# The bias of a spectral layer, added by VectorE while it reads k from PSUM instead of by products on TensorE

## The chip, the cores and the metric

The kernel runs on one core of a Trainium2 chip. The metric is the device time of one execution in microseconds (us); lower is better. Before the change three runs took 1591.71, 1594.04 and 1594.58 us, median 1594.04.

## The reference

The kernel computes a spectral layer and a mixture of experts behind it. Of 8 batches with 2496 tokens of 256 channels, it takes the real Fourier transform along the tokens, multiplies the spectrum by a complex matrix, adds a complex bias, shrinks towards zero, transforms back, and sends each token through the one of 8 experts that its gate prefers. What matters here is the complex product with its bias:

```python
X = np.fft.rfft(x, axis=1)
Xr, Xi = (X.real.astype(np.float32), X.imag.astype(np.float32))
Yr = Xr @ w_r - Xi @ w_i + b_r
Yi = Xr @ w_i + Xi @ w_r + b_i
Yr = np.sign(Yr) * np.maximum(np.abs(Yr) - lam, 0.0)
Yi = np.sign(Yi) * np.maximum(np.abs(Yi) - lam, 0.0)
y = np.fft.irfft(Yr + 1j * Yi, n=x.shape[1], axis=1)
```

## The kernel before, in words

The Fourier transform of length 2496 is done in two steps of lengths 39 and 64 (`fwd_a`, `fwd_b`), with a turn through device memory between them (`spec_dram`), and the inverse likewise (`inv_b`, `inv_a`). Each batch's spectrum is cut into 10 pieces of 128 rows, so that the spectral stage has 80 iterations, one `mix` each (`spectral`, L399). The complex product is done with three real ones: k = (Xr + Xi) w_r, and two others with (w_i - w_r) and -(w_i + w_r), to which k is added. Each of them is made of six TensorE instructions of 256 columns in the type fp32r, because operands are split into a high and a low part (`sh`, `sl` from `halves`, L304; `wh`, `wl` from `split_constants`, L235).

In `mix` (L320), TensorE first makes the product pk in PSUM; ScalarE copies it to k in SBUF (L336); GpSimd copies one element of k to `mark` (L337), by which the scattering of finished rows to the experts is paced. Then TensorE makes the two others into one PSUM tile `pm`, each beginning with a bias product (L327): a 128x128 matrix of ones by a matrix whose row 0 holds the bias's high part and row 32 its low part, all else zero. VectorE adds `pm` and k (L343), with k repeated for the two parts. `shrink` (L346) makes the threshold out of the sum, u (the tile is called `v` in the trace).

pk lies in a ring of two PSUM buffers with the tag "yo" (`psi`), which it shares with `py`, the last product of the inverse transform (L394), and with small products of the routing (`pr`, `pn`, `pq`). `pm` and `pb`, the product of `fwd_b`, have one PSUM buffer each; k has one buffer in SBUF.

The order on TensorE, on SP's queue and, within the spectral loop, on ScalarE and VectorE is the order in which the program is written. In one iteration (L441 to L492) that is: `fwd_b` and the first part of `halves` for the piece behind, the first part of `shrink` for the piece before, the second part of `halves`, routing work (`tick`), the first part of `mix` (pk and k), `fwd_a` of the next batch, `shrink`'s second and third part with routing work between them, and the second part of `mix` (`pm` and u). In four of ten iterations (`turning`, the third to the sixth of a batch) the inverse's last step `inv_a` runs in three places of the iteration, and k comes behind `fwd_a`:

```python
            if turning:
                next(mix)
            next(small, None)
            self.tick(2 + spare)
            inverse()
```

`tick` takes up the next steps of `route` (L546), some 30 small VectorE operations per half batch, and of `table` (L626). In the last batch `spare` is 1, and more of them are taken in each iteration.

Of the kernel before, what the change touches and what calls it, by code (L numbers as in the profile page):

```python
# [10 lines left out]
F32 = mybir.dt.float32  # L11
F32R = mybir.dt.float32r
# [12 lines left out]
D = 256  # L25
# [73 lines left out]
class Kernel:  # L99
# [80 lines left out]
    def open_forward(self, st):  # L180
        tc, nc, nb = self.tc, self.nc, self.nb
        f = self.f = self.pool(st, "f", 1, side="right")
        self.xp = self.pool(st, "xp", 5, side="right")
        self.tp = self.pool(st, "tp", 6, side="right")
        self.w = self.pool(st, "w", 2, side="right")
        self.psf = self.pool(st, "psf", 1, side="right", space=PSUM)

        self.far = far = f.tile([117, 120], F32, name="far")
        self.fer = f.tile([78, 120], F32, name="fer")
        nc.sync.dma_start(far, self.c_fa)  # L190
        nc.sync.dma_start(self.fer, self.c_fe)
        self.bm = f.tile([128, K1, 128], F32, name="bm")
        self.bi = f.tile([128, K1, 128], F32, name="bi")
        self.bias = f.tile([128, 2, D], F32R, name="bias")
        self.ones = f.tile([128, 128], F32R, name="ones")
        self.xg = {}
        for q in range(6):
            self.load_x(0, q)
        nc.sync.dma_start(self.bm[:, 0:4, :], self.c_bm[:, 0:4, :])
        raw = {}  # L200
        for nm, src in (("r", self.w_r), ("i", self.w_i)):
            raw[nm] = self.w.tile([128, 2, D], F32, tag="v", name="wraw")
            nc.sync.dma_start(raw[nm], src.rearrange("(c p) n -> p c n", p=128))
        self.wh, self.wl = {}, {}
        self.raw = raw
        self.braw = self.w.tile([33, 2, D], F32, tag="y", name="braw", bufs=6)
        for h, b in ((0, self.b_r), (1, self.b_i)):
            for q in (0, 32):
                nc.gpsimd.dma_start(self.braw[q:q + 1, h, :], b.rearrange("(o n) -> o n", o=1))
        self.nlam = f.tile([128, 1], F32, name="nlam")  # L210
        nc.vector.memset(self.nlam, -LAM)

        nc.gpsimd.dma_start(self.gar, self.c_ga)
        for c in range(2):
            nc.gpsimd.dma_start(self.iw[:, c, c * 128:c * 128 + 8], self.w_gate[c * 128:(c + 1) * 128, :])
        nc.gpsimd.dma_start(self.ids, self.c_ids)
        nc.gpsimd.dma_start(self.score, self.c_score)
        nc.gpsimd.dma_start(self.base, self.c_base)
        nc.gpsimd.dma_start(self.ltri_f, self.c_ltri)
        nc.gpsimd.dma_start(self.tcol, self.c_tcol)  # L220
        nc.gpsimd.memset(self.z[:, :, 64:66, :], 0.0)
# [13 lines left out]
    def split_constants(self):  # L235
        nc, f, raw = self.nc, self.f, self.raw
        ws = self.w.tile([128, 2, D], F32, tag="r", name="wsum")
        wd = self.w.tile([128, 2, D], F32, tag="r", name="wdif")
        nc.vector.tensor_sub(wd, raw["i"], raw["r"])
        nc.vector.scalar_tensor_tensor(out=ws, in0=raw["i"], scalar=-1.0, in1=raw["r"], op0=ALU.mult, op1=ALU.subtract)  # L240
        raw = {"r": raw["r"], "d": wd, "s": ws}
        zero = self.w.tile([128, 2, D], F32, tag="y", name="zero", bufs=6)
        nc.vector.memset(zero, 0.0)
        nc.vector.tensor_copy(self.bias, zero)
        nc.vector.tensor_scalar_add(self.ones, zero[:, 0, 0:128], 1.0)
        bh = self.w.tile([33, 2, D], F32R, tag="y", name="bh", bufs=6)
        nc.scalar.copy(self.bias[0:1], self.braw[0:1])
        nc.scalar.copy(bh[32:33], self.braw[32:33])
        nc.vector.tensor_sub(self.bias[32:33], self.braw[32:33], bh[32:33])
        for nm in ("s", "d", "r"):  # L250
            self.wh[nm] = f.tile([128, 2, D], F32R, name="wh" + nm)
            self.wl[nm] = f.tile([128, 2, D], F32R, name="wl" + nm)
            nc.scalar.copy(self.wh[nm], raw[nm])
            nc.vector.tensor_sub(self.wl[nm], raw[nm], self.wh[nm])
        nc.scalar.copy(self.gh, self.gar)
        nc.vector.tensor_sub(self.gl, self.gar, self.gh)
        for c in range(2):
            nc.vector.tensor_copy(self.iw[:, c, 8 - 8 * c:136 - 8 * c], self.ident)
        nc.vector.tensor_copy(self.ltri, self.ltri_f)
# [60 lines left out]
    def mix(self, b, s):  # L320
        nc = self.nc
        sh, sl = self.ss.pop((b, s))

        def product(nm, slot, to):
            i = 0 if nm == "r" else 1
            if i:
                nc.tensor.matmul(to, self.ones, self.bias[:, 1 if nm == "d" else 0, :], start=True, stop=False)  # L327
            for c in range(2):
                for a, ww in ((sh, self.wh), (sh, self.wl), (sl, self.wh)):
                    nc.tensor.matmul(to, a[:, c, slot, :], ww[nm][:, c, :], start=i == 0, stop=i == (5 if nm == "r" else 6))  # L330
                    i += 1

        pk = self.psi.tile([128, 512], F32, tag="yo", name="pk")
        product("r", 2, pk[:, :D])
        k = self.w.tile([128, D], F32, tag="k", name="k", bufs=1)
        nc.scalar.copy(k, pk[:, :D])  # L336
        self.paced = nc.gpsimd.tensor_copy(self.mark, k[0:1, 0:1])  # L337
        yield
        p = self.psf.tile([128, 2, D], F32, tag="m", name="pm", bufs=1)
        product("d", 0, p[:, 1, :])  # L340
        product("s", 1, p[:, 0, :])
        u = self.w.tile([128, 2, D], F32, tag="v", name="v")
        nc.vector.tensor_add(u, p, k.unsqueeze(1).broadcast_to((128, 2, D)))  # L343
        self.us[b, s] = u

    def shrink(self, b, s):  # L346
# [52 lines left out]
    def spectral(self, fwd):  # L399
# [41 lines left out]
        for it in range(n):  # L441
# [28 lines left out]
            if not turning:  # L470
                next(mix)
            for a in first[it]:
                self.fwd_a(*a)
            if turning:
                next(mix)
# [3 lines left out]
            next(small, None)  # L479
            self.tick(1 + spare)  # L480
            next(mix, None)
            inverse()
            self.tick(1 + spare)
# [474 lines left out]
```

## Time and profile before

| | |
|---|---|
| median of three runs | 1594.04 us (1591.71 to 1594.58) |
| profiled execution | 1596.27 us, span 1594.4 us |
| granted TensorE clock, mean | 0.987 of 2.4 GHz |
| TensorE, recorded as busy | 1531.1 us |
| VectorE | 1245.3 us |
| ScalarE | 1077.7 us |
| GpSimd | 529.1 us |

Busy time is a union of the recorded intervals; matmuls are pipelined and overlap, so TensorE's share says little of how near it is to its own rate, and the distance of starts has to be read. PE is TensorE's matmul, PEld its weight load, DVE is VectorE, ACT ScalarE, POOL GpSimd. In a row of the timeline, what stands in brackets is the idle time of the engine before that instruction, and what ended it.

### The profile page before, as it was taken

The page shows a single profiled execution, that of the slowest core. Times are in us where ns is not written, and L with a number is a line of the kernel's source. Part 1 is how long each engine was busy: PE and PEld are TensorE (multiplying, and loading weights), DVE is VectorE, ACT ScalarE, POOL GpSimd, SP SyncE. Part 2 cuts the span into 40 slices and gives each one's busy share as a digit, 9 for nine tenths or more (in the row PEclk, how much of TensorE's full clock was granted, in tenths as well). Part 3 has the DMA queues.
Part 4 walks back from the last instruction along what each step waited for, and adds up shares of the span by engine and source line. Part 5 has one row for each costly group of instructions (what it writes and reads, how often), then busy time and mean ns, then how long its engine had stood idle before and what let it go on. Part 6 is the DMA issues. An engine that isn't in the chain of part 4 may idle for free.

```text
span 1594.4 us, 35844 instructions
## 1 busy us (share of the span) xinstructions
PE 1531.1 (96%) x10963; PEld 1409.5 (88%) x10963; DVE 1245.3 (78%) x2680; ACT 1077.7 (68%) x2257; POOL 529.1 (33%) x462
## 2 busy tenths in 40 slices
PE   5999999999989798899999999999999999999997
PEld 2899898999979787789999999999999999999996
DVE  2577687777757786878888888888888888888886
ACT  2677777777756566566767676767676767676765
POOL 3002432415141433713232323333333332333332
PEclk8999999999999999999999999999999999999999
DMA  8843554636352314243213123213123213223110
GB/s 266 231 139 114 170 150 130 181 110 202 109 158 86 94 35 123 74 111 98 49 48 101 45 48 97 49 48 97 48 48 96 48 49 96 50 55 88 45 48 20
DMA packets 182962, 153.55 MB, mean 96 GB/s; under 512 B 120474, under 2 KB 154176, under 8 KB 182509
## 3 DMA queue, kind: packets, MB, share of 16 engines
q1 hardware_dynamic: 162829, 107.17, 25.9%
q0 software_dynamic: 19936, 44.04, 8.4%
q8 instruction: 89, 1.46, 0.4%
q14 instruction: 108, 0.88, 0.2%
HBM read 243.07 MB, written 66.37 MB: 194 GB/s over the span
## 4 chain that ended last, share of the span: by engine, by line
issue 41%; PE 32%; POOL 18%; DVE 4%; ACT 2%; DMA 2%; POOLq 0%; SPq 0%; another core or an unknown queue 0%; DVEq 0%; ACTq 0%
POOL out L881 17%; PE pm L330 7%; PE pz L380 5%; PE pb L300 4%; PE pv L369 4%; PE py L394 4%; PE pa L276 4%; PE pk L330 3%; PE pm L327 1%; DMA wraw<-w_r 1%; POOL xs_dram L612 1%; DVE y L356 0%; DMA x<-x 0%; POOLq L881 0%; ACT yb L395 0%
## 5 line engine op out<-in xcount | busy, mean ns | idle before, releaser
L881 POOL DMA_INDIRECT out<-o,row x154 | 299.0, 1942 | 577.3 <-DVE o L879 537.4
L871 PE MATMUL po<-h,hh 128*128 128x512 f32 x1312 | 462.4, 396 | 0.1
L833 PE MATMUL ph<-xh,h 128*128 128x256 f32 x1312 | 373.3, 285 | 6.0 <-issue 2.5
L833 PE MATMUL ph<-xh,l 128*128 128x256 f32 x1312 | 372.8, 284 | 1.0 <-DVE l L774 0.7
L833 PE MATMUL ph<-xl,h 128*128 128x256 f32 x1312 | 372.3, 284 | 0.0
L838 ACT ACTIVATE hh<-ph 128x512 fp32r<-128x512 f32 x328 | 195.9, 598 | 240.7 <-PE ph L833 230.2
L839 DVE SCALAR_TENSOR_TENSOR hl<-ph,hh 128x512 fp32r<-128x512 f32 x328 | 226.7, 691 | 139.8 <-ACT hh L838 126.9
L868 PE MATMUL po<-h,hl 128*128 128x256 f32 x1148 | 322.2, 281 | 0.2 <-DVE hl L839 0.2
L871 PEld LDWEIGHTS po<-h,hh 128*128 128x128 f32 x1312 | 241.6, 188 | 44.7 <-ACT hh L838 0.4
L833 PEld LDWEIGHTS ph<-xh,h 128*128 128x128 f32 x1312 | 252.1, 192 | 7.5 <-issue 3.2
L833 PEld LDWEIGHTS ph<-xh,l 128*128 128x128 f32 x1312 | 252.4, 192 | 5.3 <-DVE l L774 1.1
L833 PEld LDWEIGHTS ph<-xl,h 128*128 128x128 f32 x1312 | 252.3, 192 | 0.0
L868 PEld LDWEIGHTS po<-h,hl 128*128 128x128 f32 x1148 | 217.4, 189 | 4.3 <-DVE hl L839 0.5
L774 DVE TENSOR_TENSOR l<-r,h 128x512 fp32r<-128x512 f32 x332 | 206.9, 684 | 4.0 <-DMA xr<-xs_dram 1.7
L789 DVE TENSOR_TENSOR h<-r,h 128x512 fp32r<-128x512 f32 x332 | 207.1, 684 | 1.1 <-ACT h L788 0.9
L612 POOL DMA_INDIRECT xs_dram<-yb,pos x176 | 179.9, 1022 | 82.5 <-issue 59.3
L773 ACT CAST h<-r 128x512 fp32r<-128x512 f32 x332 | 180.8, 618 | 2.8 <-DMA r<-moe_w 2.8
L788 ACT CAST h<-r 128x512 fp32r<-128x512 f32 x332 | 180.5, 618 | 0.6 <-DMA r<-moe_w 0.6
L337 POOL COPY mark<-k 1x1 f32<-1x1 f32 x80 | 24.4, 305 | 356.1 <-ACT k L336 352.5
L356 DVE SCALAR_TENSOR_TENSOR y<-v,r 64x256 f32<-64x256 f32 x320 | 133.7, 418 | 6.1 <-ACT r L350 1.6
L313 DVE TENSOR_TENSOR su<-re,pb 128x256 f32<-128x256 f32 x80 | 33.7, 421 | 93.5 <-ACT sh L312 49.4
L380 PE MATMUL pz<-iw,z 128*120 128x136 f32 x704 | 97.1, 281 | 4.5 <-DVE zl L386 3.7
(180 smaller groups left out, 2861.1 us busy)
## 6 DMA issues: line engine op xcount, KB each, us to landing
r<-moe_w SPq DMA_DIRECT2D x178, 512.0 KB
r<-moe_w SPq DMA_DIRECT2D x632, 128.0 KB
spec_dram<-ae SPq DMA_DIRECT2D x88, 240.0 KB
t<-spec_dram SPq DMA_DIRECT2D x160, 128.0 KB
xq<-xs_dram SPq DMA_DIRECT2D x312, 64.0 KB
x<-x SPq DMA_DIRECT2D x40, 384.0 KB
x<-x SPq DMA_DIRECT2D x40, 84.0 KB
xs_dram<-yb,pos POOLq DMA_INDIRECT x176
```

Source lines behind the costliest of these rows:

```text
L380: nc.tensor.matmul(p[:120, c * 136:(c + 1) * 136], self.z[:, c, 3 * g:3 * g + 3, :].rearrange("p j a -> p (j a)"), self.iw[:, c, :], start ...
L612: i = nc.gpsimd.indirect_dma_start(out=self.xs[:, :], out_offset=bass.IndirectOffsetOnAxis(ap=pos[:n, g:g + 1], axis=0), in_=y[:n, g, 0:XW ...
L773: nc.scalar.copy(hi[:, c, s], v)
L774: nc.vector.tensor_sub(lo[:, c, s], v, hi[:, c, s])
L788: nc.scalar.copy(hi[:, s, :], v)
L789: nc.vector.tensor_sub(lo[:, s, :], v, hi[:, s, :])
L833: nc.tensor.matmul(p[:, i, :], a[:, c, f * 128:(f + 1) * 128], v[:, c, :], start=m == 0, stop=m == 5)
L838: nc.scalar.activation(hh[:, s, :], p, AF.Relu)
L839: nc.vector.scalar_tensor_tensor(out=hl[:, s, :], in0=p, scalar=0.0, in1=hh[:, s, :], op0=ALU.max, op1=ALU.subtract)
L868: nc.tensor.matmul(p[:, :D], hl[:, f - 1, hs], w2[:, f - 1, 0, :], start=False, stop=False)
L871: nc.tensor.matmul(p, hh[:, f, hs], w2[:, f].rearrange("p a d -> p (a d)"), start=f == 0, stop=f == 7)
L881: i = nc.gpsimd.indirect_dma_start(out=self.out[:, :], out_offset=bass.IndirectOffsetOnAxis(ap=at[h], axis=0), in_=o[:, h, :], in_offset=N ...
```

## The change

The bias is laid out over all 128 partitions as a 128 x 2 x 256 tile by two DMAs that repeat a row. The bias products and the matrix of ones are gone, with what prepared them. VectorE reads pk from PSUM, repeated for the two parts, adds the bias tile, and writes a k of two parts; ScalarE's copy is gone. The later addition of `pm` and k reads the two-part k.

```diff
-        self.bias = f.tile([128, 2, D], F32R, name="bias")
-        self.ones = f.tile([128, 128], F32R, name="ones")
+        self.bias = f.tile([128, 2, D], F32, name="bias")
...
-        self.braw = self.w.tile([33, 2, D], F32, tag="y", name="braw", bufs=6)
         for h, b in ((0, self.b_r), (1, self.b_i)):
-            for q in (0, 32):
-                nc.gpsimd.dma_start(self.braw[q:q + 1, h, :], b.rearrange("(o n) -> o n", o=1))
+            nc.gpsimd.dma_start(self.bias[:, h, :], b.rearrange("(o n) -> o n", o=1).broadcast_to((128, D)))
...
-        zero = self.w.tile([128, 2, D], F32, tag="y", name="zero", bufs=6)
-        nc.vector.memset(zero, 0.0)
-        nc.vector.tensor_copy(self.bias, zero)
-        nc.vector.tensor_scalar_add(self.ones, zero[:, 0, 0:128], 1.0)
-        bh = self.w.tile([33, 2, D], F32R, tag="y", name="bh", bufs=6)
-        nc.scalar.copy(self.bias[0:1], self.braw[0:1])
-        nc.scalar.copy(bh[32:33], self.braw[32:33])
-        nc.vector.tensor_sub(self.bias[32:33], self.braw[32:33], bh[32:33])
...
         def product(nm, slot, to):
-            i = 0 if nm == "r" else 1
-            if i:
-                nc.tensor.matmul(to, self.ones, self.bias[:, 1 if nm == "d" else 0, :], start=True, stop=False)
+            i = 0
             for c in range(2):
                 for a, ww in ((sh, self.wh), (sh, self.wl), (sl, self.wh)):
-                    nc.tensor.matmul(to, a[:, c, slot, :], ww[nm][:, c, :], start=i == 0, stop=i == (5 if nm == "r" else 6))
+                    nc.tensor.matmul(to, a[:, c, slot, :], ww[nm][:, c, :], start=i == 0, stop=i == 5)
                     i += 1
...
-        k = self.w.tile([128, D], F32, tag="k", name="k", bufs=1)
-        nc.scalar.copy(k, pk[:, :D])
-        self.paced = nc.gpsimd.tensor_copy(self.mark, k[0:1, 0:1])
+        k = self.w.tile([128, 2, D], F32, tag="k", name="k", bufs=1)
+        nc.vector.tensor_add(k, pk[:, :D].unsqueeze(1).broadcast_to((128, 2, D)), self.bias)
+        self.paced = nc.gpsimd.tensor_copy(self.mark, k[0:1, 0, 0:1])
...
-        nc.vector.tensor_add(u, p, k.unsqueeze(1).broadcast_to((128, 2, D)))
+        nc.vector.tensor_add(u, p, k)
```

On VectorE, in the fourth iteration with `inv_a` of the third batch, where the routing's running sums (`scan`, `sb`) stand; before:

```order
L317 TENSOR_TENSOR sl<-su,sh 128x2x128
L582 TENSOR_TENSOR scan_101<-scan_100 117x88
L582 TENSOR_TENSOR scan_102<-scan_101 117x88
L582 TENSOR_TENSOR scan_101<-scan_102 117x88
L582 TENSOR_TENSOR scan_102<-scan_101 117x88
L588 CAST sb<-scan_102 117x8
L356 SCALAR_TENSOR_TENSOR y<-v,r 64x256 x2
L386 TENSOR_TENSOR zl<-pz,zh 120x272 x2
```

and in the changed kernel (its line numbers are lower by up to 13):

```order
L306 TENSOR_TENSOR sl<-su,sh 128x2x128
L569 TENSOR_TENSOR scan_101<-scan_100 117x88
L569 TENSOR_TENSOR scan_102<-scan_101 117x88
L569 TENSOR_TENSOR scan_101<-scan_102 117x88
L569 TENSOR_TENSOR scan_102<-scan_101 117x88
L575 CAST sb<-scan_102 117x8
L323 TENSOR_TENSOR k<-pk,bias 128x512
L343 SCALAR_TENSOR_TENSOR y<-v,r 64x256 x2
L373 TENSOR_TENSOR zl<-pz,zh 120x272 x2
```

The addition that makes k stands behind the routing's five operations and ahead of `y`.

On ScalarE, the same place before, where the copy stood behind `ae`, the copy of `fwd_a`'s product:

```order
L350 ACTIVATE r<-v,nlam 128x512
L316 CAST sh<-su 128x2x128
L284 COPY ae<-pa 120x512
L336 COPY k<-pk 128x256
L385 CAST zh<-pz 120x272 x2
```

In the changed kernel the row of k is missing there, and the others stand as they did.

On VectorE in the last batch, second iteration, the changed kernel's k stands behind the sums of the tile table (the last of them is shown):

```order
L648 TENSOR_TENSOR te<-tcol,pfb 128x8
L651 TENSOR_REDUCE fin<-te 128x1
L323 TENSOR_TENSOR k<-pk,bias 128x512
L343 SCALAR_TENSOR_TENSOR y<-v,r 64x256 x2
L653 TENSOR_SCALAR fin<-fin 128x2
```

Before, `y` followed `fin` there, and k was made on ScalarE.

## Rows read from the trace of the kernel before

**Rows 1.** The page, share of busy time and number of instructions of each engine over the whole span.

```profile
PE 1531.1 (96%) x10963; PEld 1409.5 (88%) x10963; DVE 1245.3 (78%) x2680; ACT 1077.7 (68%) x2257; POOL 529.1 (33%) x462
```

**Rows 2.** Busy time by stretch of the span: the stretch in us, its length, busy us of PE, PEld, DVE, ACT and POOL (with the number of instructions), then granted TensorE clock, the DMA engines' share and GB/s. The beginning, the third batch, and the last.

```profile
0.00:40.00 40.00, 23.45 (x69) 10.46 (x70) 11.24 (x30) 9.21 (x16) 12.37 (x29) 0.84 0.83 267
...
170.00:241.00 71.00, 70.13 (x541) 64.31 (x540) 53.46 (x148) 51.47 (x127) 24.86 (x33) 1.00 0.50 149
...
529.00:605.00 76.00, 64.70 (x507) 61.07 (x508) 58.29 (x183) 45.41 (x112) 29.00 (x37) 0.98 0.18 55
```

**Rows 3.** Timeline of TensorE in the fourth iteration with `inv_a` of the third batch: start in us, length in us, instruction. First the end of pk, then the second `py`, then the first and the last of fourteen `pm` products in a row.

```profile
207.31 0.29 PE L330 MATMUL pk<-whr,sl 128*128 128x256 f32 x1
...
208.74 0.29 PE L394 MATMUL py<-zh,gh 120*117 120x272 f32 x1
...
209.11 0.29 PE L327 MATMUL pm<-bias,ones 128*128 128x256 f32 x1
...
210.66 0.28 PE L330 MATMUL pm<-whs,sl 128*128 128x256 f32 x1
```

**Rows 4.** Timeline of VectorE in a plain iteration, the second one of the third batch.

```profile
170.46 0.69 DVE L343 TENSOR_TENSOR v<-pm,k 128x512 f32<-128x512 f32 x1 [1.00 <-PE pm L330]
172.23 0.42 DVE L313 TENSOR_TENSOR su<-re,pb 128x256 f32<-128x256 f32 x1 [1.08 <-ACT sh L312]
...
175.47 0.69 DVE L343 TENSOR_TENSOR v<-pm,k 128x512 f32<-128x512 f32 x1 [0.26 <-issue]
177.24 0.42 DVE L313 TENSOR_TENSOR su<-re,pb 128x256 f32<-128x256 f32 x1 [1.08 <-issue]
```

**Rows 5.** Timelines of TensorE and VectorE in the last batch: the places where TensorE begins after an idle time, and what stands on VectorE there.

```profile
546.45 0.58 PE L394 MATMUL py<-zh,gh 120*117 120x272 f32 x1 [5.37 <-ACT k L336]
...
547.40 0.84 DVE L356 SCALAR_TENSOR_TENSOR y<-v,r 64x256 f32<-64x256 f32 x2
...
568.07 0.38 PE L394 MATMUL py<-zh,gh 120*117 120x272 f32 x1 [0.72 <-ACT k L336]
...
577.73 0.39 PE L394 MATMUL py<-zh,gh 120*117 120x272 f32 x1 [0.18 <-DVE rb L598]
...
588.15 0.17 PE L592 MATMUL pr<-sb,ltri 117*117 117x8 bf16 x1 [1.43 <-DVE sb L588]
...
589.01 0.69 DVE L343 TENSOR_TENSOR v<-pm,k 128x512 f32<-128x512 f32 x1
589.62 0.41 DVE L313 TENSOR_TENSOR su<-re,pb 128x256 f32<-128x256 f32 x1
```

**Rows 6.** Groups of instructions of VectorE and ScalarE from 45 to 605 us: line, engine, operation, tiles, shapes, number, then busy us and mean ns of one, then idle us of the engine before them and what ended it.

```profile
L343 DVE TENSOR_TENSOR v<-pm,k 128x512 f32<-128x512 f32 x80 | 55.1, 689 | 37.9 <-PE pm L330 18.8 <-issue 4.6 <-PE pz L380 4.5
...
L313 DVE TENSOR_TENSOR su<-re,pb 128x256 f32<-128x256 f32 x78 | 32.8, 421 | 80.8 <-ACT sh L312 36.7 <-PE pz L380 26.5 <-ACT re L311 8.0
...
L336 ACT COPY k<-pk 128x256 f32<-128x256 f32 x79 | 33.6, 426 | 3.6 <-remote 2.0 <-PE pk L330 1.0 <-PE pz L380 0.4
```

**Rows 7.** Timeline of ScalarE around k, in the third and then in the fourth iteration with `inv_a` of the third batch.

```profile
198.41 0.28 ACT L562 ACTIVATE ex<-lg 117x88 f32<-117x88 f32 x1 [1.22 <-DVE lg L560]
198.59 0.57 ACT L284 COPY ae<-pa 120x512 f32<-120x512 f32 x1
199.06 0.38 ACT L336 COPY k<-pk 128x256 f32<-128x256 f32 x1
...
207.74 0.38 ACT L336 COPY k<-pk 128x256 f32<-128x256 f32 x1
```

**Rows 8.** Timeline of VectorE in the fourth iteration with `inv_a` of the third batch.

```profile
207.74 1.10 DVE L582 TENSOR_TENSOR scan<-scan 117x88 f32<-117x88 f32 x4
208.87 0.17 DVE L588 CAST sb<-scan 117x8 bf16<-117x8 f32 x1
208.95 0.84 DVE L356 SCALAR_TENSOR_TENSOR y<-v,r 64x256 f32<-64x256 f32 x2
```

**Rows 9.** Timelines in the third iteration with `inv_a` of the third batch: VectorE's last `lg`, and the second `py` on TensorE.

```profile
198.13 0.25 DVE L560 TENSOR_TENSOR lg<-lg,mx 117x88 f32<-117x88 f32 x1
...
199.49 0.38 PE L394 MATMUL py<-zh,gh 120*117 120x272 f32 x1 [0.76 <-ACT k L336]
```

**Rows 10.** Timelines of VectorE and TensorE in the eighth and ninth iteration of the third batch. Between the first and the last of its rows VectorE has no row with an idle time in brackets.

```profile
220.43 0.42 DVE L313 TENSOR_TENSOR su<-re,pb 128x256 f32<-128x256 f32 x1 [1.09 <-PE pk L330]
...
225.50 0.68 DVE L343 TENSOR_TENSOR v<-pm,k 128x512 f32<-128x512 f32 x1
...
226.66 0.17 DVE L588 CAST sb<-scan 117x8 bf16<-117x8 f32 x1
...
231.66 0.42 DVE L313 TENSOR_TENSOR su<-re,pb 128x256 f32<-128x256 f32 x1 [0.92 <-ACT re L311]
...
227.80 0.17 PE L592 MATMUL pr<-sb,ltri 117*117 117x8 bf16 x1
...
227.88 0.37 PE L327 MATMUL pm<-bias,ones 128*128 128x256 f32 x1
```

**Rows 11.** Timeline of GpSimd at the beginning, and the summary of ScalarE's k over the whole span (length of one in ns, least, median and greatest; first and last start).

```profile
1.36 0.71 POOL L209 DMA_DIRECT2D braw<-b_r  x1 [0.40 <-issue]
...
2.99 0.97 POOL L209 DMA_DIRECT2D braw<-b_i  x2
...
L336 ACT COPY k<-pk x80: 353/446/474, 42.9 to 604.4; 128x256 f32<-128x256 f32 x80
```

## The prediction

> **What bounds the kernel now.** I read the page's shares of busy time first [rows 1], then the same by stretch [rows 2], then TensorE's and VectorE's instructions in order of time, last the waits. The change touches the spectral stage alone, about 45 to 605 us of the span of 1594.4: `mix` runs there, 80 times. In an undisturbed batch (170 to 241 us) TensorE's records cover 70.13 of 71 us, VectorE's 53.46, ScalarE's 51.47 [rows 2]. Busy shares of overlapping matmuls prove little, so I looked at starts: in the run of `pm` products the first starts at 209.11 and the fourteenth at 210.66, thirteen steps of 0.119 us without a hole, although each is recorded as 0.28 us [rows 3]. TensorE works through its queue at its own rate; VectorE and ScalarE catch up in gaps, as the 1.0 us and 1.1 us before `v` and `su` [rows 4]. So in most of the stage time is TensorE's. The exception is the last batch, 529 to 605 us: TensorE covers only 64.70 of 76 us while VectorE has 58.29 [rows 2], and TensorE is seen waiting for it [rows 5].
>
> **The change, part by part.**
>
> *Removed from TensorE:* 160 bias products, two in each `mix`. They are worth their spacing, not their recorded length: 160 x 0.119 = **19.0 us** gained, 0.238 in each iteration [rows 3]. The granted clock is 1.00 in that stretch, the 2.4 GHz level [rows 2]. The Trainium skill (TensorE: Matmul & The Clock Gate, "Wait — 56ns, not 53.3ns?") gives the columns over 2.4 GHz plus 2.5 ns, which for 256 columns I estimate as 109 ns: 17.5 us in place of 19.0, and 1.5 us less gain in the sum; the row shows 0.119, so it decides.
>
> *Moved from ScalarE to VectorE:* k. ScalarE loses 80 copies of 0.43 us; VectorE gains 80 additions. No row has this very operation. The nearest is `v<-pm,k`, the same 128x512 with one operand in PSUM and one repeated: 689 ns [rows 6], and I take that, since the output count and the two operands agree. The lower end is 421 ns, `su`, also an addition from PSUM but over 256 (if the repeated reading cost nothing); the upper end is two such, 842 ns. What the next VectorE instruction sees is less than the recorded length: `v` starts at 589.01 and the next at 589.62, so 0.61 us of the engine [rows 5]. 80 x 0.61 = 49 us more for VectorE. Where does that lie? In a plain iteration VectorE idles 0.26 + 1.08 us between 172.23 and 177.24 [rows 4], a period of 5.01 us that the removed products shorten by 0.24; 0.61 + 0.24 fits under 1.34. There I cost it at nothing; its cover is this idle time, and if that were gone each iteration would cost up to 0.61.
>
> *Who waits for k.* k reads pk out of a ring of two PSUM buffers ("yo") that `py` also uses. In the four iterations of a batch in which `inv_a` runs, pk takes one, the first `py` behind it the other, and the second `py` waits until k has read pk. That is the place where the position in a queue decides:
> - Fourth of those iterations: ScalarE made k at 207.74 to 208.12 [rows 7] and the second `py` at 208.74 needed no wait [rows 3]. VectorE now has k behind four `scan` additions and the cast `sb`, so it can begin at 208.95, where `y` began [rows 8], and ends at 208.95 + 0.69 = 209.64; `py` starts about 0.05 later (as after ScalarE's k, which ended at 199.44, for 199.49 [rows 7, 9]), 209.69 in place of 208.74: 0.95 us lost, in six batches **5.7 us**. With the ends above, 4.1 to 6.6.
> - Third: ScalarE's k was held by `ex` and `ae` until 199.06, and `py` waited 0.76 us for it [rows 7, 9]. VectorE's k follows `lg` and ends at 198.38 + 0.69 = 199.07, not 199.44: 0.37 us gained, six times, **2.2 us**.
> - First and second: k's end moves by under 0.2 us; nothing.
>
> *The busiest plain iterations* (seventh to ninth of a batch, with the routing work): VectorE has no gap from 220.43 to 231.66 but the 0.92 us at the end [rows 10]. Two ks add 1.22 us there, and TensorE moves up 0.24 to 0.48. `sb` would end at 226.83 + 0.61 = 227.44, and TensorE wants it at 227.80 - 0.24 = 227.56 [rows 10]: just in time. Cost 0, bound 0.6 per batch. This is the thinnest margin of the forecast.
>
> *Last batch:* two routing jobs and the tile table share it, with more of them in each iteration, and TensorE already waits. k now follows the table's sums and ends at 547.40 + 0.69 = 548.09, where `py` got it at 546.45: 1.7 us. In the next three marked places it ends or pushes what TensorE waits for (k itself, `rb`, `sb`) by about 0.6 each [rows 5]. Together **3.5 us** lost; ends 0 (these waits are absorbed) and 7 (VectorE's ten ks at 0.61 plus part of the first again).
>
> *Beginning:* four DMAs of 1 KB into two rows become two that repeat 256 numbers over 128 partitions, 256 KB; four small VectorE operations, two ScalarE copies go. The bias is needed first at about 42.9 us, its DMAs are issued at 1.36 to 3.96 [rows 11]. Cost 0; the upper bound is the 256 KB at the rate of that stretch, 267 GB/s [rows 2], 1.0 us. One fewer row on GpSimd is nothing; its `mark` now reads VectorE's k, which only shifts when three rows may be scattered, and the scatters have room.
>
> *ScalarE* is relieved of 34 us [rows 6]; no wait of TensorE ends on it there but the k above, so I add nothing.
>
> **Sum:** -19.0 + 5.7 - 2.2 + 3.5 = -12.0 us. The profiled execution took 1596.27 us, so 1584.3; the median of the runs shown is 1594.04, 2.2 lower, so I say **1582.0 us**. The expert stage behind is not touched and moves up as a block.
>
> **Rivals.**
> A. *No new waits.* VectorE always arrives in time: -19.0 - 2.2 = -21.2, 1572.8 us. For it: the gaps of the plain iterations [rows 4]. Against: the order on VectorE in the fourth iteration leaves no way around `scan`.
> B. *VectorE's queue becomes the pace* where routing work is queued: seventh to ninth iteration of six batches and the ten of the last, 28 iterations, each paying 0.61 instead of gaining 0.24. 28 x 0.61 = +17.1, the other 52 gain 12.4, the two `py` terms are +5.7 - 2.2: +8.2, **1602.2 us**, slower. It decides if VectorE's 0.92 us of idle time [rows 10] is used up and the delay reaches the single PSUM buffer of `pm`, which `v` must have read before the next `pm`. For it: 1.22 us do not fit in 0.92. Against: the iterations behind have gaps of over 1 us, and `pm` begins more than 1 us after the `v` before it. The Trainium skill (Perfetto Trace Analysis, "Optimizing Scalar/DVE Operations") advises moving work from VectorE to ScalarE when VectorE is saturated, and this change does the opposite; by that rule B is the outcome, while the trace agrees only in 529 to 605 us.
> C. *No gain.* What TensorE saves it waits again at the next hand-over, as at the end of a `pm` whose `v` comes later: about 1594. Against it are the hole-free starts [rows 3].
>
> One thing hangs over all: TensorE stood still 5.37 us at 546.45 for no reason of the program's order [rows 5]. Such a pause may come or go, so I widen by about one on either side.
>
> **How the numbers follow.** Forecast 0.58, A 0.13, B 0.20, C 0.09. About 0.2% (3.2 us) is what a measurement of this kernel can tell from no change. Faster by over that: forecast nearly whole, and A: 0.70. Within: C and the edges of the forecast: 0.13. Slower: B less its better edge: 0.17. The forecast's own range is 1575 to 1590 (the ends of its terms); with A below and most of B above, 1573 to 1600.
>
> **What would show it.** Right: no `bias` product, `pm` groups of 12; the k addition near 0.69 us; in 170 to 241 us the period shorter by about 1.8 us; a TensorE wait of about 1 us for k at the fourth `inv_a` iteration, none of 0.76 at the third; the last batch no shorter. Wrong: TensorE waits for `v` or `sl` in plain iterations (B), the batch shortened by the full 2.4 (A), or not at all (C).

## The result, and the profile of the changed kernel

The changed kernel took 1602.27 us (median of 7 runs, 1596.88 to 1607.15), the kernel before 1592.27 us beside it (7 runs): a ratio of 1.0063, 95% interval 1.0041 to 1.0085, **slower by 10 us**. I had said 1582.0 and 0.70 for faster. The profiled execution took 1605.27 us, with a span of 1603.4.

The edit took the bias products out and moved k. On the page (columns as in [rows 1]) TensorE has 160 products fewer:

```profile
PE 1519.4 (95%) x10803; PEld 1390.0 (87%) x10803; DVE 1288.3 (80%) x2756; ACT 1057.0 (66%) x2175; POOL 536.8 (33%) x460
```

In the groups from 45 to 605 us (columns as in [rows 6]) k takes 685 ns, near the 0.69 us that I had taken:

```profile
L323 DVE TENSOR_TENSOR k<-pk,bias 128x512 f32<-128x512 f32 x80 | 54.8, 685 | 3.6 <-PE pm L317 2.3 <-PE pa L265 0.7 <-PE pk L317 0.4
```

The timelines of TensorE and VectorE in the third and fourth iterations with `inv_a` of the third batch answer to [rows 3, 7 to 9]. The wait of 0.76 us at the third is down to 0.31; I had said 0.37 less, it is 0.45 less. At the fourth there is a new one, but for `yb`, ScalarE's copy, and not for k:

```profile
198.14 0.68 DVE L323 TENSOR_TENSOR k<-pk,bias 128x512 f32<-128x512 f32 x1
198.88 0.39 PE L381 MATMUL py<-zh,gh 120*117 120x272 f32 x1 [0.31 <-DVE k L323]
208.10 0.69 DVE L323 TENSOR_TENSOR k<-pk,bias 128x512 f32<-128x512 f32 x1
208.52 0.39 PE L381 MATMUL py<-zh,gh 120*117 120x272 f32 x1 [0.47 <-ACT yb L382]
```

What I had not foreseen stands in the stretches (columns as in [rows 2]). In 168 to 173 us VectorE works 0.98 and ScalarE 0.61 of 5 us; in 598 to 617 us, at the end of the loop, TensorE only 9.07 of 19:

```profile
168.00:173.00 5.00, 5.00 (x40) 4.51 (x38) 0.98 (x2) 0.61 (x2) 2.71 (x3) 1.00 0.85 247
598.00:617.00 19.00, 9.07 (x62) 7.14 (x62) 7.91 (x18) 7.30 (x14) 12.57 (x14) 0.87 0.26 80
```

VectorE's and TensorE's timelines there show the largest hole: the last product of `pm` starts at 603.36, `v` waits until 614.11, and `pv` behind it starts after 7.65 us of TensorE's idle time; the `pv` before it had waited 2.13.

```profile
603.36 0.28 PE L317 MATMUL pm<-whs,sl 128*128 128x256 f32 x1
...
604.17 0.69 DVE L323 TENSOR_TENSOR k<-pk,bias 128x512 f32<-128x512 f32 x1 [2.27 <-PE pm L317]
604.78 1.73 DVE L343 SCALAR_TENSOR_TENSOR y<-v,r 64x256 f32<-64x256 f32 x4
614.11 0.69 DVE L330 TENSOR_TENSOR v<-pm,k 128x512 f32<-128x512 f32 x1 [7.61 <-remote]
...
616.65 2.05 PE L356 MATMUL pv<-bi,y 128*128 128x128 f32 x8 [7.65 <-DVE y L343]
```

The kernel before has such holes too, elsewhere. I compared the start of each iteration's first pk product in both traces: after 15 iterations the changed kernel is 2.5 us ahead, after 60 it is 5.1 behind, after 65, where two holes of before have passed, 3.0 ahead, after 79 1.5 behind, and at the first expert product 10.1 behind.

Three theories follow. **Theory 1**: VectorE's order makes TensorE wait in the loop, more than forecast. **Theory 2**: these pauses decide, in which VectorE and ScalarE stand though TensorE goes on; in the profiles they lie where GpSimd scatters rows one behind the other, 0.3 us apart, and the change may move those runs together, since `mark` now follows VectorE's k. **Theory 3**: VectorE's k is held because its single buffer must first be read by `mark`, behind those rows.

### The profile page after: what moved, and what is told of

It is laid out like the page before. It is cut to its first block, busy times and chain, and to the rows that moved or that the text cites. A ratio compares the mean times of both kernels' runs of the same rounds, so it can differ in the third digit from the quotient of the medians.

```text
span 1603.4 us, 35687 instructions
## 1 busy us (share of the span) xinstructions
PE 1519.4 (95%) x10803; PEld 1390.0 (87%) x10803; DVE 1288.3 (80%) x2756; ACT 1057.0 (66%) x2175; POOL 536.8 (33%) x460
## 3 DMA queue, kind: packets, MB, share of 16 engines
q8 instruction: 88, 1.44, 0.4%
## 5 line engine op out<-in xcount | busy, mean ns | idle before, releaser
L868 POOL DMA_INDIRECT out<-o,row x154 | 303.7, 1972 | 571.2 <-DVE o L866 546.2
L599 POOL DMA_INDIRECT xs_dram<-yb,pos x176 | 185.1, 1052 | 92.8 <-issue 42.3
L356 PEld LDWEIGHTS pv<-bi,y 128*128 128x128 f32 x640 | 81.0, 193 | 25.0 <-issue 11.0
L289 PE MATMUL pb<-bm,t 128*128 128x128 f32 x640 | 86.5, 279 | 15.7 <-DMA t<-spec_dram 10.4
```

The lines of the kernel that those rows point to most:

```text
L599: i = nc.gpsimd.indirect_dma_start(out=self.xs[:, :], out_offset=bass.IndirectOffsetOnAxis(ap=pos[:n, g:g + 1], axis=0), in_=y[:n, g, 0:XW ...
L868: i = nc.gpsimd.indirect_dma_start(out=self.out[:, :], out_offset=bass.IndirectOffsetOnAxis(ap=at[h], axis=0), in_=o[:, h, :], in_offset=N ...
```

## Experiments

Ratios are to the kernel before, run beside each kernel on the same chip. On chip 13 ran nobias, kdve, a_spread and b_spread; on chip 7 a_again, b_again, kb2 and latebias; on chip 6 nbk, kpool, prlater and a_third, and later a_burst and a_fifth; on chip 0 a_fourth, a_spread_2, best and best_spread. The number of the chip that gave the result isn't on record. Below it is called the first chip, but a state of that chip can't be told from a state of that hour.

### The parts of the change, one at a time

```diff
 nobias (from before): products out, the bias isn't added at all
-            if i: nc.tensor.matmul(to, self.ones, self.bias[...], start=True, stop=False)
 kdve (from before): products stay
-        nc.scalar.copy(k, pk[:, :D])
+        nc.vector.tensor_copy(k, pk[:, :D])
 nbk: both edits, the bias isn't added at all
```

nobias. 

> The kernel before without its 160 bias products, k still copied by ScalarE; the bias is left out of what is computed. Theory 1 (VectorE's new place for k makes TensorE wait) has the 160 x 0.119 = 19.0 us for itself here, since no work comes to VectorE: about 1573 us, ratio 0.988. Theory 2 (what decides is where TensorE's completion signals come late while GpSimd sends rows without a gap, and any shift of phase moves those pauses) allows anything from 1573 to 1592 here, and its profile must show pauses of VectorE and ScalarE of 1.5 us and more together at other places than before, each within a run of rows without a gap.

Measured: 1558.05 us against 1577.05, 0.9885 (0.9866 to 0.9904).

kdve. 

> The kernel before with k copied from PSUM by VectorE (128x256) and the bias products kept. Theory 1: TensorE waits for k in the fourth and third inv_a iterations and for sb behind it, and pays some 10 us with nothing given back: about 1602 us, ratio 1.006. The forecast on record (+5.7, -2.2, +3.5) gives about 1600. Theory 2: the waits of the order are largely hidden and the time is that of before, 1592, give or take the pauses (5 us).

Measured: 1577.97 us, 1.0010 (0.9998 to 1.0021).

nbk. 

> The kernel before without bias products and with k copied by VectorE (128x256), the bias left out of what is computed: the changed kernel but for the size of one operation (128x256 copied, where the changed kernel adds 128x512, 0.68 us) and the transfer of the bias. Alone, taking the products out gave 0.9885 (-18.1 us) and moving k gave 1.001 (+1.6 us). If the two simply add up, 0.9895 (1560 us of 1577). Theory 1 (VectorE's queue is what gives the saving back: with TensorE 2.4 us shorter in ten iterations, every operation more on VectorE is waited for): well above that, 0.993 to 0.996, with sb and y waited for in each batch. Then what is left to the changed kernel's 0.9976 is the second 256 columns.

Measured: 1566.10 us against 1577.46, 0.9913 (0.9898 to 0.9928).

The products are worth what I said: 18.1 us by the ratio, and in the profiles of nobias and b_again (below) 18.95 us from the pk of iteration 0 to that of 79, 0.120 for each of the 158 products between. Moving a 128x256 copy to VectorE costs 1.6 us with the products (not clear of noise; 3.8 in the loop of the profile) and 4.4 without (6.1 in the loop), less than kdve's and nbk's expectations. From nbk's 0.9913 to the mean of the changed kernel's four runs below, 0.9986, are another 11.5 us: by subtraction the width of the addition and the later beginning take the larger part of the saving. And the kernel before took 1577 us, not 1592: in the profiles of the four kernels on chip 13 there is no such pause.

### The two kernels on other chips

No edit: b_again is the kernel before, the others are the changed kernel.

a_again. 

> The changed kernel, unchanged, beside the kernel before on the same chip. In the runs so far the kernel before took 1577 us where it had taken 1592 to 1594, and the profiles of the four kernels run there have none of the pauses in which VectorE and ScalarE both stand. Theory 2 in its new form (the pauses are a state of the chip or the run, and cost the two kernels unlike amounts): no pause over 1.2 us between 100 and 640 us where the kernel before has none, and a ratio of 0.999 to 1.002. Theory 1 (the order's waits alone make the changed kernel slower): 1.006 again, with no pause in its profile.

b_again. 

> The kernel before, unchanged, for its profile on this chip: ratio 1.000. Theory 2: none of the five pauses (14.8 us) of its first profile if the time is near 1577 us, and all of them or as many if it is near 1592.

a_third. 

> The changed kernel again, on whatever chip this is. If the kernel before takes about 1577 us here, 0.9976 as on the second chip, with no pause; if it takes 1592 or more, the pauses are back in both profiles and the ratio is 1.004 to 1.008 as at first.

a_fourth. 

> The changed kernel on a further chip, for the comparison with the next three. Before at about 1577 us: 0.998 and no pauses. Before at 1592 or more: 1.004 to 1.008, with pauses of VectorE and ScalarE in runs of rows without a gap.

a_fifth. 

> The changed kernel beside it. Before at about 1577 us: 0.998 to 1.000 and no pauses; before at 1592: 1.004 to 1.008, with pauses.

Measured: b_again 1576.68 us, 0.9998 (0.9987 to 1.0009). The changed kernel: 1572.45, 0.9976 (0.9965 to 0.9987); 1573.73, 0.9986 (0.9975 to 0.9997); 1576.48, 0.9999 (0.9985 to 1.0013); 1573.68, 0.9984 (0.9971 to 0.9997). Mean 0.9986: **2.2 us faster**; a_fourth by itself shows no difference. There is no such pause in any of the five profiles, and the +10 us of the result came in none of these four runs, on three chips.

The twin of the stretch at 168 us, first the chip of the result, then a_again (timelines of VectorE, ScalarE, GpSimd and TensorE; a_again is 0.23 us earlier):

```profile
166.56 1.73 DVE L343 SCALAR_TENSOR_TENSOR y<-v,r 64x256 f32<-64x256 f32 x4
169.98 0.69 DVE L330 TENSOR_TENSOR v<-pm,k 128x512 f32<-128x512 f32 x1 [1.70 <-PE pb L289]
...
172.38 0.37 ACT L300 COPY re<-pb 128x256 f32<-128x256 f32 x1 [4.75 <-PE pa L265]
...
167.57 1.15 POOL L599 DMA_INDIRECT xs_dram<-yb,pos  x1 [0.50 <-issue]
...
168.16 0.28 PE L317 MATMUL pm<-whs,sl 128*128 128x256 f32 x1
```

```profile
166.33 1.73 DVE L343 SCALAR_TENSOR_TENSOR y<-v,r 64x256 f32<-64x256 f32 x4
168.24 0.69 DVE L330 TENSOR_TENSOR v<-pm,k 128x512 f32<-128x512 f32 x1 [0.18 <-PE pm L317]
...
169.18 0.37 ACT L300 COPY re<-pb 128x256 f32<-128x256 f32 x1 [1.78 <-PE pb L289]
...
167.35 1.15 POOL L599 DMA_INDIRECT xs_dram<-yb,pos  x1 [0.51 <-ACT ae L273]
...
167.92 0.28 PE L317 MATMUL pm<-whs,sl 128*128 128x256 f32 x1
```

The last product of `pm` starts at 168.16 in the one and 167.92 in the other, GpSimd's rows lie at the same places, the DMA engines are as busy in both (0.85 in 168 to 173 us, 0.91 in a_again's 167.77 to 172.77), and what starts late waits for TensorE: `v` by 1.5 us, `re` by 3.0. At the loop's end a_again's `v` starts without a wait at 588.02, where the first chip's waited 7.61 us, although GpSimd sends rows there too, from 584.42 to 597 with no gap over 1 us. The kernel before has such a pair: the `v` of iteration 59 waits 3.75 us on the first chip and 0.22 in b_again.

```profile
453.14 0.69 DVE L343 TENSOR_TENSOR v<-pm,k 128x512 f32<-128x512 f32 x1 [3.75 <-PE pa L276]
```

```profile
447.82 0.69 DVE L343 TENSOR_TENSOR v<-pm,k 128x512 f32<-128x512 f32 x1 [0.22 <-PE pm L330]
```

The spans, split at pk of iterations 0 and 79 and at the first expert product (us, from the four traces):

| stretch | before, first chip | b_again | changed, first chip | a_again |
|---|---|---|---|---|
| to the loop | 40.8 | 40.8 | 42.2 | 42.0 |
| iterations 0 to 79 | 557.5 | 544.7 | 557.6 | 542.6 |
| to the first expert product | 35.6 | 31.8 | 44.2 | 31.6 |
| the rest | 960.5 | 958.5 | 959.4 | 954.9 |
| span | 1594.4 | 1575.8 | 1603.4 | 1571.1 |

By these profiles the first chip costs the kernel before 18.6 us and the changed one 32.3, 13.7 more, of which 8.8 behind the loop. By the medians it is 12.2: the changed kernel is 10.0 slower there and 2.2 faster elsewhere. Part of it is TensorE's clock. Where the changed kernel on the first chip stands longest, 6.7 us for `zh` and then 7.65 for `y`, the granted clock falls to its lower level of 1.2 GHz, for 10.2 us each time (columns as in [rows 2]):

```profile
540.40:550.60 10.20, 5.99 (x26) 5.69 (x27) 7.23 (x40) 3.41 (x9) 2.44 (x4) 0.50 0.11 37
612.10:622.30 10.20, 4.91 (x20) 4.62 (x21) 3.01 (x7) 3.74 (x7) 1.38 (x2) 0.50 0.30 98
```

The kernel before has two such stretches between 45 us and the first expert product as well, of 6.8 and 3.4 us (467.6 to 474.4 and 546.1 to 549.5). The first pauses come at full clock (1.00 in 168 to 173 us), so the clock follows them and doesn't make them. The rest, 954.9 to 958.5 us, differs as much between profiles of the same kernel, and with the clock: behind the first expert product a_again (954.9) and a_third (955.1) have 3.4 us at the lower level, a_fifth (956.3) 6.8, a_fourth (958.1) and b_again (958.5) 10.2.

### Are the pauses made by GpSimd's runs of rows?

```diff
 a_spread, b_spread, a_spread_2: one row behind k, y and u (two behind u in the last batch)
-            self.send(4 if late else 3)
+            self.send(1) ... self.pace(self.last_y[0:1, 0, 0:1]); self.send(1)
+            ... self.pace(self.us[b, s][0:1, 0, 0:1]) ... self.send(2 if late else 1)
 a_burst: no mark, all eleven rows of a half in one run
-        self.paced = nc.gpsimd.tensor_copy(self.mark, k[0:1, 0, 0:1])
-            self.send(4 if late else 3)
+            self.send(11)
```

a_spread. 

> The changed kernel with each iteration's three or four rows set apart: one behind k, one behind y, one or two behind u, each with a copy of mark of its own, where all stood behind the copy of k. Theory 2: the pauses of VectorE and ScalarE together (14 us in the changed kernel's profile, 4.6 of them at the loop's end) are gone or shorter than 1 us, and the time is 8 to 14 us below the changed kernel, 1588 to 1594. Theory 1: the rows don't matter, 1602 us, ratio to before 1.006, with the waits of py, pr and pv for VectorE unchanged.

b_spread. 

> The kernel before with the rows set apart in the same way. Theory 2: the five pauses of before's profile (449, 461, 472, 527 and 598 us, 14.8 us together) are gone, and the time falls by 5 to 12 us, to 1580 to 1587. Theory 1: no difference, 1592.

a_spread_2. 

> The changed kernel with the rows set apart. If the pauses are back on this chip and come of long runs of rows, this one has none and is 10 to 25 us below the changed kernel; if they are back and don't come of the rows, it has as many. Without pauses on this chip: within 0.15% of the changed kernel, as on the first chip of the experiments (0.9997).

a_burst. 

> The changed kernel with all the rows of a half sent in one run, unpaced (no copy to mark; 11 rows of 1.3 us one behind the other). If long runs of rows delay TensorE's signals on any chip: pauses of VectorE and ScalarE of several us in each of the 16 runs of rows, and a time at least 20 us above the changed kernel's. If it takes the first chip's state as well: no pause here, and a time within 0.3% of the changed kernel's.

Measured: a_spread 0.9997 (0.9984 to 1.0011), b_spread 1.0006 (0.9993 to 1.0019), a_spread_2 0.9989 (0.9979 to 1.0000), a_burst 0.9982 (0.9969 to 0.9995). None has a pause, but neither has the changed kernel on these chips (on the first of them only a_spread ran, beside kdve, nobias and b_spread). The first two expectations counted on pauses that weren't there, so the spacing decided nothing. a_burst decides one point: eleven rows in 14 us (147.3 to 161.5) stop no engine on chip 6. Theory 2 is right that the pauses made the result slower; that runs of rows alone bring them about is refuted. On the first chip they lie in such runs; what else it takes was not found, since it didn't come again, and the spacing couldn't be tried on it.

### Two small theories, and another place for the bias

```diff
 kb2
-        k = self.w.tile([128, 2, D], F32, tag="k", name="k", bufs=1)
+        k = self.w.tile([128, 2, D], F32, tag="k", name="k", bufs=2)
 latebias: the two transfers of the bias on SP, behind self.turn(0, 2)
-            nc.gpsimd.dma_start(self.bias[:, h, :], ...)
+            self.nc.sync.dma_start(self.bias[:, h, :], ...)
 kpool
-        nc.vector.tensor_add(k, pk[...], self.bias)
+        nc.scalar.copy(kr, pk[:, :D])
+        self.paced = nc.gpsimd.tensor_add(k, kr.unsqueeze(1).broadcast_to((128, 2, D)), self.bias)
```

kb2. 

> The changed kernel with two buffers for k, so that VectorE's add of k needn't wait until GpSimd's copy to mark has read the former k. Theory 3 (VectorE is held by that wait behind GpSimd's rows): TensorE's waits for y and sb are shorter and the time falls by 3 us or more below the changed kernel's. Theory 1: VectorE waits for pk, not for mark; no change against the changed kernel (within 0.1%).

latebias. 

> The changed kernel with the two bias transfers (256 KB) issued on SP's queue behind the third turn of the first batch, at about 36 us, instead of ahead of the constants on GpSimd's. The beginning is then that of before: pk of iteration 0 at 40.8 us instead of 42.2, and the time 1.3 us below the changed kernel's (0.999 of it); if the beginning is hidden further on, no change.

kpool. 

> The changed kernel with k copied by ScalarE (128x256) as before and the bias added from SBUF to SBUF by GpSimd (128x512, in the place of its copy to mark), no bias work on VectorE or TensorE. Theory 1: VectorE is as free as in the kernel without bias; if GpSimd's add is done before v needs it, 0.989 to 0.991. If GpSimd's rows are ahead of the add, v is late by one or more rows (1.3 us each) in the iterations that send rows, and TensorE waits for y behind it: above 1.00.

Measured: kb2 0.9995 (0.9983 to 1.0007), no gain over a_again's 0.9976 beside it; theory 3 falls. latebias 0.9996 (0.9983 to 1.0009): pk of iteration 0 comes at 39.87, 2.1 us earlier than a_again's 42.00, but the turns behind the bias on SP come later, `pb` waits 2.0 us for `t`, and iteration 5 starts at 69.40 against 69.07. kpool 1.0145 (1.0129 to 1.0160): GpSimd's addition takes 1.39 us, twice VectorE's 0.69 (the group below), and VectorE's and TensorE's waits for `sb`, `zl` and `kr` grow to 14.4, 7.5 and 7.4 us.

```profile
L325 POOL TENSOR_TENSOR k<-kr,bias 128x512 f32<-128x512 f32 x79 | 109.7, 1389 | 287.2 <-ACT kr L323 229.9 <-DVE lg L555 57.1
```

### The waits of the order taken away

```diff
 prlater, best, best_spread
-        for _ in range(10 if b == self.nb - 1 else 5):
+        for _ in range(10 if b == self.nb - 1 else 7):
 best, best_spread: the bias as one row, spread once by TensorE
-            nc.gpsimd.dma_start(self.bias[:, h, :], b....broadcast_to((128, D)))
+            nc.gpsimd.dma_start(self.braw[:, h, :], b.rearrange("(o n) -> o n", o=1))
+        nc.tensor.matmul(pb, self.row1, self.braw..., start=True, stop=True)
+        nc.vector.tensor_copy(self.bias..., pb)
```

prlater. 

> The changed kernel with the product pr two ticks further back in the routing's order (7 steps behind sb, where it was 5; the last batch unchanged). Theory 1: TensorE's wait of 0.8 us for sb in each of the first six batches is gone, and if nothing else is waited for in its place the time falls by 4 to 5 us (ratio to before 0.9945 to 0.995). If VectorE's own queue is the pace in those iterations, y or k is waited for instead and the ratio stays 0.9976.

best. 

> The changed kernel with pr two ticks further back (0.9936 by itself) and the bias loaded as one row of 2 KB and spread over the partitions once by a TensorE product with ones, in place of 256 KB of transfers. Theory: the beginning is that of before again (pk of iteration 0 at 40.8 us, not 42.0), worth 1.2 us on top: 0.993. If the first iterations' waits hide the later beginning: 0.9936.

best_spread. 

> The same with the rows set apart as well. No pauses on this chip: the same as the kernel without (within 0.15%). Pauses on this chip: faster than it by what the pauses cost there.

Measured: prlater 1567.89 us against 1577.46, **0.9936** (0.9922 to 0.9950), 7.9 us below the changed kernel beside it (a_third) by the ratios and 5.3 in the profiles at the first expert product. best 1565.61 against 1576.67, **0.9928** (0.9914 to 0.9942), the fastest kernel here that adds the bias; over prlater it isn't settled by the ratios, but its profile has pk of iteration 0 at 40.60 (prlater 42.89) and the first expert product at 609.34 (611.42). best_spread 0.9944 (0.9930 to 0.9957): spacing the rows adds nothing here.

The sums of TensorE's waits from 45 to 620 us (us in total, times, longest), first b_again, then a_again, then prlater:

```profile
PE py L394 <- ACT k L336: 5.5, 7, 1.0
PE py L394 <- DVE zl L386: 5.3, 2, 3.7
PE pr L592 <- DVE sb L588: 2.1, 2, 1.4
PE py L394 <- ACT yb L395: 1.5, 2, 1.0
```

```profile
PE pr L579 <- DVE sb L575: 7.7, 7, 2.3
PE py L381 <- ACT yb L382: 6.6, 11, 1.3
PE py L381 <- DVE zl L373: 4.8, 3, 3.0
PE py L381 <- DVE k L323: 1.9, 6, 0.4
PE pv L356 <- DVE y L343: 1.2, 7, 0.2
```

```profile
PE py L381 <- ACT yb L382: 7.1, 12, 1.3
PE py L381 <- DVE zl L373: 4.8, 3, 3.0
PE pr L579 <- DVE sb L575: 2.4, 1, 2.4
```

`sb` was waited for twice before and seven times after; two ticks further back, once. TensorE now waits for `yb` where it had waited for k.

## Why the prediction was wrong

Two things make up the miss of 20 us: the kernel itself gains 2 us instead of 12, and the first chip's pauses hit the changed kernel 12 to 14 us harder (the kernel before took 1.8 us less beside the result than when I predicted, which hides that much). The first by its steps, from the distances between the iterations' first pk products in b_again and a_again, with 0.24 us of products added back in each iteration. The numbers per batch are means of iterations 20 to 60; with -2.38 for the products they make -0.65, and the four batches gained 2.69, 0.67 each:

| step | forecast | measured |
|---|---|---|
| bias products | -19.0 | -18.95 (nobias) |
| `py`, fourth iteration with `inv_a` | +5.7 | 0.73 x 6 = +4.4 |
| `py`, third | -2.2 | -0.50 x 6 = -3.0 |
| `py`, first | 0 | 0.22 x 6 = +1.3 |
| busiest plain iterations | 0 | 1.28 x 5 + 3.8 = +10.2 |
| last batch (iterations 70 to 79) | +3.5 | +3.7 |
| beginning | 0 | +1.2 |
| sum | -12.0 | -1.15 |

By stretch, changed against before: iterations 0 to 20, forecast -4.2, measured -2.7; 20 to 60, -7.2 and -2.7; 60 to 79, -0.4 and +3.2; to the first expert product -12.0 and -1.1. So the largest single error of the sum is the row of the busiest plain iterations.

**The step that failed first is "the busiest plain iterations ... just in time. Cost 0, bound 0.6 per batch".** I set `sb`'s end at 227.44 against 227.56 wanted [rows 10]; that counts one k ahead of `sb`, though I had named two, and TensorE's gain of one iteration. With both ks and both iterations' gain the same rows give 226.83 + 1.22 = 228.05 against 227.80 - 0.48 = 227.32, 0.73 us late. The k of the iteration before (212.05) isn't covered by VectorE's idle time: the 1.09 us ahead of `su` are a wait for ScalarE's `sh`, and ScalarE had itself waited for VectorE's `lg`, 2.65 us where b_again has 2.05. `lg` comes later by about one k, 0.6 us, and with it `ex`, `re`, `sh` and `su`. From 217.82 to 235.61 VectorE then shows no idle time; in b_again it had 0.91 us there ahead of the ninth iteration's `su`, and three ks of 0.61 don't fit. TensorE waits at `pr` and then again for `y`, 0.84 and 0.44 us per batch, 1.28 together, outside the bound. The timelines of VectorE, ScalarE and TensorE in a_again, then ScalarE's `ex` in b_again:

```profile
212.05 0.68 DVE L323 TENSOR_TENSOR k<-pk,bias 128x512 f32<-128x512 f32 x1
...
216.76 0.28 ACT L549 ACTIVATE ex<-lg 117x88 f32<-117x88 f32 x1 [2.65 <-DVE lg L547]
...
217.82 0.42 DVE L302 TENSOR_TENSOR su<-re,pb 128x256 f32<-128x256 f32 x1 [1.09 <-ACT sh L301]
...
219.82 0.69 DVE L323 TENSOR_TENSOR k<-pk,bias 128x512 f32<-128x512 f32 x1
...
224.65 0.17 DVE L575 CAST sb<-scan 117x8 bf16<-117x8 f32 x1
...
235.61 0.43 DVE L306 TENSOR_TENSOR sl<-su,sh 128x256 fp32r<-128x256 f32 x1 [0.16 <-ACT sh L305]
...
224.87 0.22 PE L579 MATMUL pr<-sb,ltri 117*117 117x8 bf16 x1 [0.60 <-DVE sb L575]
...
233.86 0.71 PE L356 MATMUL pv<-bi,y 128*128 128x128 f32 x4 [0.17 <-DVE y L343]
```

```profile
218.54 0.28 ACT L562 ACTIVATE ex<-lg 117x88 f32<-117x88 f32 x1 [2.05 <-DVE lg L560]
```

In iteration 68, in the batch before the last, the same wait for `sb` is 2.32 us (0.66 in b_again), and behind it the granted clock falls to 1.2 GHz for 3.4 us: TensorE's products start every 0.215 us instead of 0.119, which costs another 1.5. With the wait for `y` behind it that batch pays 3.8 here. a_fifth, whose clock didn't fall there, loses 1.65 in that iteration. (Columns as in [rows 2].)

```profile
505.90:509.40 3.50, 3.48 (x18) 3.48 (x19) 3.41 (x8) 2.55 (x6) 1.38 (x3) 0.52 0.34 111
```

prlater confirms the step: with only `pr` moved, iterations 0 to 60 gain 12.0 us against b_again where my forecast was 11.4 and the changed kernel gained 5.4. nbk confirms the reason: with copies of half the width TensorE waits only 0.24 to 0.34 us per batch for `sb` up to iteration 59, and not for `y`. This is rival B's mechanism, VectorE's queue as the pace, in two iterations of a batch instead of three; but the delay reached TensorE at `pr` and `pv`, and not by way of `pm` as B had it (a_again shows no wait for `v`). I had given B 0.20. That B's 1602.2 us is the time that was measured is luck: it counted no pauses, and without them the kernel took 1572 to 1576. The rule of the Trainium skill (Perfetto Trace Analysis, "Optimizing Scalar/DVE Operations") that I set beside it, to move work off a saturated VectorE, was the better guide in these iterations; in the other plain ones the trace agrees with the forecast, each being 0.23 to 0.25 us shorter.

*Fourth `py`:* the place was right, the mechanism not. k stands where I put it, but the second `py` starts before k's record ends (205.25 + 0.69), so it doesn't wait for k. It waits for ScalarE's `yb`, which empties the first `py`, 0.47 us, and 0.73 by the distances of pk. So it stands in that one's buffer here. Before, it started at 208.74 [rows 3], ahead of `yb` at 208.94, and so didn't. VectorE, ScalarE and TensorE in a_again, then ScalarE before:

```profile
205.25 0.69 DVE L323 TENSOR_TENSOR k<-pk,bias 128x512 f32<-128x512 f32 x1
...
205.23 0.39 ACT L382 COPY yb<-py 117x272 f32<-117x272 f32 x1
...
204.56 0.38 PE L381 MATMUL py<-zh,gh 120*117 120x272 f32 x1
...
205.67 0.38 PE L381 MATMUL py<-zh,gh 120*117 120x272 f32 x1 [0.47 <-ACT yb L382]
```

```profile
208.94 0.76 ACT L395 COPY yb<-py 117x272 f32<-117x272 f32 x2
```

The two kernels thus use the ring's buffers in different order, and I had carried the old one over. I had also said that no wait of TensorE ends on ScalarE but that for k. Before's trace has one of 0.6 us for `yb`, and a_again has eleven, 6.6 us together.

*Last batch:* the size was right, in part by luck. From iteration 70 to 79 a_again loses 1.3 us where nobias gains 2.4, 3.7 in all for 3.5 forecast. But the waits are only in part the ones named: `sb` 2.28 us (1.44 in b_again), `yb` up to 1.31, `n` 0.91. And the granted clock has its part on both sides: it is at the lower level for some 3.4 us behind the wait for `sb` in a_again, and for 6.8 around a wait of 3.72 us in b_again (the second row is from there).

```profile
574.40:577.70 3.30, 3.30 (x18) 3.30 (x17) 2.97 (x10) 2.10 (x5) 1.95 (x2) 0.50 0.36 109
```

```profile
536.40:541.70 5.30, 5.30 (x24) 5.30 (x25) 3.93 (x10) 2.41 (x6) 0.00 (x0) 0.50 0.00 0
```

*Beginning:* 1.2 us, where my upper bound was 1.0. ScalarE's wait for the weights shows it: it isn't longer, but ends 1.15 us later; with the bias loaded as one row (best) it ends 0.4 earlier than before, at 23.34. b_again, then a_again:

```profile
23.78 0.62 ACT L253 CAST whr<-wraw 128x512 fp32r<-128x512 f32 x1 [6.67 <-DMA wraw<-w_r]
```

```profile
24.93 0.62 ACT L242 CAST whr<-wraw 128x512 fp32r<-128x512 f32 x1 [6.46 <-DMA wraw<-w_r]
```

*The pauses:* I saw one, 5.37 us at 546.45 [rows 5], held it to have no reason in the program's order, and widened the range by "about one" either way. In b_again `py` waits 3.72 us for `zl` in that iteration, so most of it belongs to the order. The real ones stood in the same trace as idle time of VectorE and ScalarE together (449, 461, 472, 527 and 598 us, 14.8 us in all), and I never listed the time in which both stand. That term, put at about nothing on balance, is the second step that failed: it measured 12 to 14 us against the changed kernel, as the medians and the table of spans show. Why the changed kernel pays more on the first chip isn't shown; its runs of rows at the loop's end are one candidate, with the lower clock behind the waits.

*What held:* the products' spacing of 0.119. My estimate of 109 ns from the Trainium skill (TensorE: Matmul & The Clock Gate, "Wait — 56ns, not 53.3ns?") would have given 17.2 us for the 158 products in which the profiles show 18.95; the measurement decides.

## What to carry to other kernels

Work moved to an engine is paid where that engine's queue has no idle time to spare over several iterations: add up the moved work over the whole stretch, not up to the next hand-over. Idle time in which the engine waits for a second engine is no cover when that one waits for the first. If the work doesn't fit, move the waiting instruction first (two ticks on `pr` gave back 5 to 8 of the 10 us that were missing). Before pricing an edit, list where all consumers of an engine stand at once while it goes on: here such time was worth as much as the edit, and only runs on other chips told the two apart. The same two kernels stood at 1.006 in one comparison and at 0.998 to 1.000 in four others.

## What the runs showed of the hardware

- On the occasion of the result the kernel before took 1592 us, on four known chips 1577, at the same mean granted clock (0.987 in the two profiles of it). There, instructions that wait for TensorE stood up to 7.6 us while GpSimd and, in the pause at 168 us, TensorE too went on. The trace of the changed kernel has fewer records of signals there than a_again's: 1324 against 1409 of TensorE's, but also 2239 against 2448 of VectorE's and 1928 against 2078 of ScalarE's. So the loss isn't particular to TensorE. Matmul ends are modelled, and whether products, signals or only the recording suffered stays open.
- TensorE's granted clock fell to 1.2 GHz behind or within some of its waits of 2.3 to 7.7 us, for 3.4 to 10.2 us, and products of 256 columns then started every 0.215 us instead of every 0.119. A wait of 3.03 us in a_again (to 534.87) left it at the upper level.
- A 128x512 addition from SBUF took GpSimd 1.39 us, and VectorE 0.69 us with one operand in PSUM.
- Eleven scattered rows 0.3 us apart, 14 us together, delayed no engine on the chip where they were tried.
